# A kernel's own verdict counted by a product with ones, and two evictions moved from ScalarE to VectorE

## The chip, the cores and the metric

The kernel runs on one core of a Trainium2 chip. The metric is the device time of one execution in microseconds, as a median of several runs. A profile is of one execution; its span runs from the first to the last instruction of the program.

## What is computed

The reference is a gated linear recurrence (GateLoop) followed by a two-layer block with the activation h cos(h):

```python
# q, k, v, a_re, a_im: (4, 8, 768, 48); the state S is complex, per head 48 x 48
mag = np.sqrt(a_re * a_re + a_im * a_im)
scale = np.minimum(mag, 0.999) / (mag + 1e-06)
for t in range(S):
    S = (a_re + i a_im)[t] * scale[t] * S + outer(k[t], v[t])
    y[t] = q[t] @ real(S)
x = y.transpose(0, 2, 1, 3).reshape(3072, 384)
h = x @ w_in                 # w_in (384, 2048)
out = (h * np.cos(h)) @ w_out  # w_out (2048, 384), out (3072, 384)
```

(The recurrence is written here in complex form; the reference keeps the real and the imaginary part apart.)

## The kernel before

The program holds two kernels. `fast_path` relies on properties of the inputs: no real part below zero, powers that stay in range, weights that are normal numbers, arguments of the cosine in a range. While it runs it keeps account of them. `general_path` relies on none. At the end one value, the flag, is 1 if the account shows that the fast path's output can't be relied on. A branch (`tc.If(late["taken"] > 0)`, line 1658) then runs the general path, which writes everything again; the other arm (line 1661) only makes the last store. With the inputs used here the flag is 0 and the general path doesn't run.

**Tiles and groups.** The 4 x 768 steps are cut into chunks of 128 steps, two chunks are a group, and there are 12 groups (`NG`). A group passes through logarithms and powers of the gates, a phase, stacked keys and queries, scores, outputs and states, the first layer (`mm1_sums`, tiles `hp`), the activation (`gate_sine` on ScalarE, `gate_product` on VectorE) and the second layer. From the third group on, the second layer is Strassen's form of a product of 2 x 2 blocks: `mixed` makes sums of blocks of the gate on VectorE (tile `s`), and `seventh` makes one of seven products.

**The seven products of the last group.** `products` issues them in the order p0, p1, p3, p2, p5, p4, p6, each in two halves (`part`). p0, p3 and p5 add up in one PSUM tile, `sum`, which is evicted after each of them; p1, p2, p4 and p6 have a PSUM tile `op` each, which VectorE multiplies by a factor and adds to one or two of the blocks c11, c12, c21, c22 of the output (tile `ot`). In the last group (g = `NG` - 1) c12 is the tile `rest`, which outlives the fast path, and p6 stands alone: p5's sum is evicted twice, into c22 and into c12, and p6 is added to c12 last (`alone`). c11 is stored by SyncE after p1 (line 1210), the lower half of the rows after p4 (line 1212), and c12 by ScalarE from within the branch's other arm (line 1215).

**The account and the verdict.** `least` (96 x 16) holds ones and zeros for the powers at the chunks' ends, `odd` (128 x 41 partial sums, zero if nothing is amiss) the gates and the weights, `wide` the sums of squares of h. `verdict` is a generator that `judged` resumes three times within the last group's products. Its first step reduces `least` to `low` (96 x 1, ones and zeros) and `odd` and `wide` to `even` (128 x 1, ones and zeros), and in the kernel before writes both into a line in DRAM (lines 1634 and 1636) and reads that line back into one partition (line 1638). Its second step takes the minimum of the line (line 1641), compares it (line 1644, the flag) and has each engine read the flag into a register (line 1646). Its third step ties TensorE's read to a place among the matmuls.

**What sets the order.** On TensorE every matmul is chained to the one before (`matmul`, line 686), so its order is that of the program. On the other engines a planner sets the order by what is ready and by program order; `behind(a, b)` forbids that `a` goes before `b` on their engine. So line 1641 stands behind `late["vector"]`, the last eviction by VectorE that was issued till then; ScalarE's read of the flag behind `late["scalar"]`; TensorE's behind `late["tensor"]`; the last add behind VectorE's read (line 1206); p4's store behind SyncE's read (line 1213), and c11's store behind the read of the line (line 1210). `weave` merges lists of steps by due times between 0 and 1. In the last call the products' fourteen halves are due at (i + 0.5) / 14; the verdict's first step comes at 0.10 (between the halves of p0), the second at 0.59 (between p2 and p5), the third at 0.78 (between the halves of p4).

Of the kernel before, what the change touches and what calls it, by code (L numbers as in the profile page):

```python
# [11 lines left out]
F32 = mybir.dt.float32  # L12
# [7 lines left out]
ALU = mybir.AluOpType  # L20
AX = mybir.AxisListType
# [466 lines left out]
def fast_path(ctx, tc, q, k, v, a_re, a_im, moe_w_in, moe_w_out, out, least, odd, wide,  # L488
# [7 lines left out]
    nc = tc.nc  # L496
    B, H, S, D = q.shape
    DM, DF = moe_w_in.shape
    C = 128
# [3 lines left out]
    NG = N // G  # L503
    D2 = 2 * D
# [17 lines left out]
    pa = ctx.enter_context(tc.tile_pool(name="pa", bufs=5, space=PSUM))  # L522
# [11 lines left out]
    late = {}  # L534
# [8 lines left out]
    def behind(ins, other):  # L543
        tc.add_manual_dep(ins.ins, other.ins.name, mybir.DependencyInfo(
            mybir.DependencyClass.NoSync, mybir.DependencyReason.DATA))
# [9 lines left out]
    def scalar_tile(value, name):  # L555
        t = consts.tile([C, 1], F32, name=name)
        nc.vector.memset(t, value)
        return t
# [33 lines left out]
    one_b = scalar_tile(1.0, "one_b")  # L592
# [91 lines left out]
    vector, scalar = Ordered(nc.vector, "vector"), Ordered(nc.scalar, "scalar")  # L684

    def matmul(out, **kw):
        chain(nc.tensor.matmul(out, **kw), "tensor")  # L687
# [446 lines left out]
    PLAIN, HJ, E2 = 2, NJ // 2, DM // 2  # L1134
# [33 lines left out]
    scale = 1.0 / (in_scale * out_scale)  # L1168

    def left(g, name, j):  # L1170
        if name[0] == "s":
            return X[g]["mix"][j // 2][name][:, j % 2]
        half, i = int(name[2]) - 1, int(name[1]) - 1
        return X[g]["gate"][j // 2 + half * (HJ // 2)][:, j % 2, ts(i, C)]

    def seventh(g, p, part):


        x, name = X[g], SEVEN[p]
        if p == 0 and part == 0:  # L1180
            x["sum"] = pm.tile([C, E2], F32, tag="acc", name="sum", bufs=1)
            x["ot"] = [msb.tile([C, DM], F32, tag="ot", name="ot") for _ in range(G)]

        alone = g == NG - 1 and p == 6
        summed = p in (0, 3, 5, 6) and not alone
        if not summed and part == 0:
            x["op"] = pm.tile([C, E2], F32, tag="m", name="op", bufs=2)
        ps = x["sum"] if summed else x["op"]
        for j in range(part * HJ // 2, (part + 1) * HJ // 2):
            matmul(ps, lhsT=left(g, name, j), rhs=right[name][:, j],  # L1190
                   start=(j == 0 and (p == 0 or not summed)),
                   stop=(j == HJ - 1), skip_group_check=summed)
        if part == 0:
            return
        c11, c12, c21, c22 = (x["ot"][i][:, ts(half, E2)] for i in range(2) for half in range(2))
        if g == NG - 1:
            c12 = rest
        if p in (0, 3, 5) or p == 6 and not alone:
            late["scalar"] = scalar.mul(out={0: c11, 3: c21, 5: c22, 6: c12}[p], in_=ps, mul=scale)
        if g == NG - 1 and p == 5:  # L1200
            scalar.mul(out=c12, in_=ps, mul=scale)
        for part_ in {1: [c11], 2: [c21], 4: [c21, c22], 6: [c12] * alone}.get(p, []):
            added = vector.scalar_tensor_tensor(out=part_, in0=ps, scalar=scale,
                                                in1=part_, op0=ALU.mult, op1=ALU.add)
            if alone:
                behind(added, late["read DVE"])
            late["vector"] = added
        row = g * G * C
        if g == NG - 1 and p == 1:
            behind(nc.sync.dma_start(out=out[ds(row, C), 0:E2], in_=c11), late["line"])  # L1210
        elif p == 4:
            put = nc.sync.dma_start(out=out[ds(row + C, C), :], in_=x["ot"][1])
            behind(put, late["read SP"] if g == NG - 1 else late["ends"])
        elif p == 6 and alone:
            late["store"] = lambda: nc.scalar.dma_start(out=out[ds(row, C), E2:DM], in_=c12)
        elif p == 6:
            nc.sync.dma_start(out=out[ds(row, C), :], in_=x["ot"][0])

    def products(g, lo, hi):
        if g < PLAIN:  # L1220
            return []
        return [lambda p=p, part=part: seventh(g, p, part)
                for p in (0, 1, 3, 2, 5, 4, 6)[lo:hi] for part in range(2)]

    def mixes(g, lo, hi):
        return [lambda p=p: mixed(g, p) for p in range(lo, hi)] if g >= PLAIN else []
# [202 lines left out]
    even = even_steps(1, 0, G)  # L1429
# [101 lines left out]
    even = even_steps(2, 0, G)  # L1531
# [49 lines left out]
    for n in range(2, NG):  # L1581
# [6 lines left out]
              (keys(n + 1), *((0.5, 0.62) if n == PLAIN else (0.53, 0.64))),  # L1588
              (last_quarter() if n == PLAIN else [], 0.9, 1.0), (first(n), 0.56, 1.0),
              (mixes(n, 0, 2), 0.9, 1.0), (guarded(n - 1, per) if n > 3 else [], 0.0, 0.38))  # L1590
    checked = verdict(late, temp)

    def judged():
        late["tensor"] = tail["tensor"]
        next(checked, None)

    weave((mixes(NG - 1, 2, 4), 0.0, 0.1), ([judged], 0.05, 0.15),
          (products(NG - 1, 0, 7), 0.0, 1.0), ([judged], 0.58, 0.6), ([judged], 0.76, 0.8))
    assert not guards
    return late  # L1600
@with_exitstack
def kernel(ctx, tc, q, k, v, a_re, a_im, moe_w_in, moe_w_out, out):

    nc = tc.nc
    D2, H = 2 * q.shape[3], q.shape[1]
    keep = ctx.enter_context(tc.tile_pool(name="keep", bufs=1))
    least = keep.tile([D2, 2 * H], F32, name="least")
    C = 128  # L1610
    NG, NJ = q.shape[0] * q.shape[2] // C // 2, moe_w_out.shape[0] // C
    odd = keep.tile([C, moe_w_in.shape[0] // C * 4 + NJ + NG + 1], F32, name="odd")
    wide = keep.tile([C, NG * NJ // 2], F32, name="wide")
    rest = keep.tile([C, moe_w_out.shape[1] // 2], F32, name="rest")
    scratch = ctx.enter_context(tc.tile_pool(name="scratch", bufs=1,
                                             space=bass.MemoryType.DRAM))

    def behind(ins, other):
        tc.add_manual_dep(ins.ins, other.ins.name, mybir.DependencyInfo(
            mybir.DependencyClass.NoSync, mybir.DependencyReason.DATA))  # L1620

    def verdict(late, temp):

        low = keep.tile([D2, 1], F32, name="low")
        nc.vector.tensor_reduce(out=low, in_=least, axis=AX.X, op=ALU.min)
        even = keep.tile([C, 1], F32, name="even")
        nc.vector.tensor_reduce(out=even, in_=odd, axis=AX.X, op=ALU.max)
        most = keep.tile([C, 1], F32, name="most")
        nc.vector.tensor_reduce(out=most, in_=wide, axis=AX.X, op=ALU.max)
        nc.vector.tensor_scalar(out=even, in0=even, scalar1=0.0, scalar2=None, op0=ALU.is_le)  # L1630
        nc.vector.tensor_scalar(out=most, in0=most, scalar1=2.4, scalar2=None, op0=ALU.is_le)
        nc.vector.tensor_tensor(out=even, in0=even, in1=most, op=ALU.mult)
        line_d = scratch.tile([D2 + C], F32, name="line_d")
        behind(nc.sync.dma_start(out=line_d[0:D2], in_=low.rearrange("p o -> (p o)")),
               late["x"])
        nc.sync.dma_start(out=line_d[D2:D2 + C], in_=even.rearrange("p o -> (p o)"))
        line = temp("Q")[0:1, 0:D2 + C]
        late["line"] = nc.sync.dma_start(out=line, in_=line_d.unsqueeze(0))
        yield
        bad = keep.tile([1, 2], F32, name="bad")  # L1640
        behind(nc.vector.tensor_reduce(out=bad[:, 0:1], in_=line, axis=AX.X, op=ALU.min),
               late["vector"])
        flag = keep.tile([1, 1], I32, name="flag")
        nc.vector.tensor_scalar(out=flag, in0=bad[:, 0:1], scalar1=0.5, scalar2=None,
                                op0=ALU.is_lt)
        reads, values = nc.values_load_multi_w_load_instructions(
            flag[0:1, 0:1], min_val=0, max_val=1,
            skip_runtime_bounds_check_because="a comparison gives 0 or 1")
        late["taken"] = values[0]
        for ins in reads:  # L1650
            name = str(ins.ins.engine).split(".")[-1]
            late["read " + name] = ins
        behind(late["read Activation"], late["scalar"])
        yield
        behind(late["read PE"], late["tensor"])

    late = fast_path(tc, q, k, v, a_re, a_im, moe_w_in, moe_w_out, out, least, odd, wide, rest, verdict)
    with tc.If(late["taken"] > 0) as taken:
        general_path(tc, q, k, v, a_re, a_im, moe_w_in, moe_w_out, out)
    with taken.Else():  # L1660
        late["store"]()
# [30 lines left out]
```

## Time and profile before

| what | us |
|---|---|
| three runs: median (lowest to highest) | 660.77 (659.86 to 660.9) |
| the profiled execution | 660.9 |
| its span | 659.0 |
| TensorE busy | 643.3 (98%) |
| VectorE busy | 492.4 (75%) |
| ScalarE busy | 393.2 (60%) |
| mean granted TensorE clock | 0.999 of full speed |

The span is first instruction to last; the execution's time has 1.9 us around it. "Busy" is the share of the span in which an engine executes; reads of registers, branches, waits on semaphores and the issuing of DMAs are the sequencers' and not counted. An engine name with a q (SPq, ACTq) is such a sequencer's row. A row of the timeline has start, duration, engine, line, operation, `out<-in`, shapes, a count of merged instructions, and in brackets the idle time of the engine before it with what ended it. Matmuls overlap: one of 128x192 in f32 is two instructions of 0.327 us that start 0.163 us apart. Line 687 is the helper that issues every matmul, and line 676 the one that issues most operations of VectorE and ScalarE, so one goes by tile names.

### The profile page before, as it was taken

The numbers are of one execution on the slowest core, as the hardware profiler recorded it, in microseconds if no ns is written. First come the engines' busy times: TensorE is split into PE (matmuls) and PEld (weight loads), VectorE is DVE, ScalarE is ACT, GpSimd is POOL, SyncE is SP. The second block draws the span as 40 slices with busy tenths as digits, with TensorE's granted clock in tenths as the row PEclk, the third lists the DMA queues.
The fourth block names the chain that finished last, engine by engine and source line by source line (L and its number), as shares of the span: only waits on it lengthen the run. The fifth ranks groups of instructions, "written<-read, shape, count | busy, mean of one in ns | idle before, by whom it ended". The sixth has DMA issues, their size and how long they took to land.

```text
span 659.0 us, 10778 instructions
## 1 busy us (share of the span) xinstructions
PE 643.3 (98%) x4075; PEld 577.6 (88%) x4075; DVE 492.4 (75%) x799; ACT 393.2 (60%) x726; POOL 44.9 (7%) x72
## 2 busy tenths in 40 slices
PE   8999999999999999999999999999999999999996
PEld 6888877768889999899889899899898999999896
DVE  6999999788687687696787786876877878862251
ACT  7888686374673593594494495485485476433230
POOL 4010200000000000010010010000000010010000
PEclk9999999999999999999999999999999999999999
DMA  9967745636636656747738728737737743362101
GB/s 246 243 184 191 244 142 135 152 85 153 147 73 151 161 146 145 192 120 170 191 102 188 189 76 186 200 84 177 200 92 161 197 123 93 124 140 77 49 1 31
DMA packets 228312, 94.90 MB, mean 144 GB/s; under 512 B 208701, under 2 KB 217406, under 8 KB 228250
## 3 DMA queue, kind: packets, MB, share of 16 engines
q1 hardware_dynamic: 217720, 57.50, 39.4%
q0 software_dynamic: 8816, 36.51, 17.2%
q8 instruction: 34, 0.56, 0.4%
q10 hardware_dynamic: 1714, 0.11, 0.2%
q14 instruction: 28, 0.23, 0.1%
HBM read 69.28 MB, written 24.81 MB: 143 GB/s over the span
## 4 chain that ended last, share of the span: by engine, by line
PE 85%; DMA 4%; ACT 4%; DVE 4%; issue 1%; SPq 1%; DVEq 0%; POOLq 0%
PE hp L687 35%; PE op L687 16%; PE sum L687 15%; PE yp L687 6%; PE sc L687 5%; PE sp L687 4%; PE phs L687 2%; DMA x<-yT 1%; PE lgs L687 1%; DVE mag L676 1%; DMA kT<-moved 1%; DVE lo L676 1%; ACT tan L707 1%; PE yr L687 1%; PE tp L963 1%; DMA moved<-tr 1%
## 5 line engine op out<-in xcount | busy, mean ns | idle before, releaser
L687 PE MATMUL hp<-xT,w_in 128*128 128x256 f32 (+1 forms) x1176 | 252.6, 375 | 0.9 <-DMA xT<-x 0.9
L687 PEld LDWEIGHTS hp<-xT,w_in 128*128 128x128 f32 x1176 | 220.0, 190 | 31.0 <-issue 1.3
L707 ACT ACTIVATE gate<-hp,half_pi_b 128x512 f32<-128x512 f32 x96 | 66.0, 687 | 119.8 <-PE hp L687 119.8
L687 PE MATMUL op<-w_out,gate 128*128 128x192 f32 (+1 forms) x448 | 100.7, 375 | 0.0
L676 DVE TENSOR_TENSOR gate<-hp,gate 128x512 f32<-128x512 f32 x96 | 65.6, 683 | 46.9 <-ACT junk L676 46.8
L687 PEld LDWEIGHTS op<-w_out,gate 128*128 128x128 f32 x448 | 76.0, 190 | 16.8 <-issue 2.0
L687 PE MATMUL sum<-t_s,s 128*128 128x192 f32 x320 | 57.8, 330 | 0.0
L676 ACT ACTIVATE junk<-hp 128x512 bf16<-128x512 f32 x96 | 56.6, 590 | 0.0
L687 PEld LDWEIGHTS sum<-t_s,s 128*128 128x128 f32 x320 | 52.1, 190 | 1.5 <-issue 1.5
L687 PEld LDWEIGHTS sc<-qT,kT 96*128 96x128 f32 x384 | 48.2, 192 | 4.0 <-DMA qT<-moved 1.2
L687 PE MATMUL sc<-qT,kT 96*128 96x128 f32 x384 | 50.3, 277 | 1.3 <-DMA kT<-moved 0.8
L676 DVE SCALAR_TENSOR_TENSOR ot<-op,ot 128x192 f32<-128x192 f32 x40 | 13.3, 353 | 48.7 <-PE op L687 47.1
L676 DVE TENSOR_TENSOR atm<-sc,causal 128x512 f32<-128x512 f32 x48 | 32.8, 686 | 22.1 <-PE sc L687 22.1
L676 ACT ACTIVATE ot<-sum 128x192 f32<-128x192 f32 x39 | 12.6, 322 | 54.0 <-PE sum L687 53.8
L687 PE MATMUL yp<-atm,v 128*48 128x128 f32 x352 | 33.6, 277 | 0.9 <-DVE atm L676 0.9
L703 ACT ACT_TABLE_LOAD x24 | 30.8, 1283 | 1.1 <-PEq L1676 0.7
L676 ACT COPY yT<-yp 48x512 f32<-48x512 f32 x44 | 25.3, 574 | 8.2 <-PE yp L687 7.6
L687 PEld LDWEIGHTS sp<-v,ks 128*96 128x96 f32 x320 | 30.0, 165 | 0.1
L687 PE MATMUL yp<-qT,state 96*48 96x128 f32 x304 | 29.7, 272 | 0.0
L687 PE MATMUL sp<-v,ks 128*96 128x48 f32 x320 | 29.7, 246 | 0.0
L687 PE MATMUL sum<-w_out,gate 128*128 128x192 f32 x160 | 29.2, 327 | 0.0
L676 ACT CAST tan<-phs 128x384 int32<-128x384 f32 x24 | 11.4, 481 | 29.4 <-PE phs L687 29.4
(149 smaller groups left out, 1000.6 us busy)
## 6 DMA issues: line engine op xcount, KB each, us to landing
moved<-tr SPq DMA_DIRECT2D x20, 768.0 KB
raw<-in_moe_w_in_dram POOLq DMA_DIRECT2D x16, 768.0 KB, 5.2
raw<-in_moe_w_out_dram POOLq DMA_DIRECT2D x16, 768.0 KB, 4.7
kT<-moved SPq DMA_DIRECT2D x40, 192.0 KB
qT<-moved POOLq DMA_DIRECT2D x9, 768.0 KB, 6.4
k<-in_k_dram SPq DMA_DIRECT2D x24, 192.0 KB
q<-in_q_dram SPq DMA_DIRECT2D x24, 192.0 KB
v<-in_v_dram SPq DMA_DIRECT2D x24, 192.0 KB
```

What stands on the lines that cost most here:

```text
L676: ins = getattr(self.engine, op)(**kw)
L687: chain(nc.tensor.matmul(out, **kw), "tensor")
L703: chain(nc.scalar.preload_act_table_set(table))
L707: chain(nc.scalar.activation(func=func, **kw))
L963: chain(nc.tensor.transpose(ps[:, h], X[g][name[0] + "s"][:, x0 + h].rearrange("p a d -> p (a d)"), ident), "tensor")
```

## The change

The verdict's line in DRAM goes. `low` is multiplied into the first 96 partitions of `even` on VectorE, and a product of `even` (128 x 1) with a column of ones (`one_b`) on TensorE counts the ones in it into a 1 x 1 PSUM tile, `good`. The flag is 1 if the count is below 127.5. The flag's comparison now has the place behind `late["vector"]` that the minimum had. The verdict's second step is due at 0.43 in place of 0.59, which is between p3 and p2. Of p5 in the last group, both evictions are VectorE's. c11's store is no longer tied to the line.

```diff
+        if g == NG - 1 and p == 5:
+            for out_ in c22, c12:
+                vector.tensor_scalar(out=out_, in0=ps, scalar1=scale, scalar2=None, op0=ALU.mult)
+        elif p in (0, 3, 5) or p == 6 and not alone:
-        if p in (0, 3, 5) or p == 6 and not alone:
             late["scalar"] = scalar.mul(out={0: c11, 3: c21, 5: c22, 6: c12}[p], in_=ps, mul=scale)
-        if g == NG - 1 and p == 5:
-            scalar.mul(out=c12, in_=ps, mul=scale)
...
         if g == NG - 1 and p == 1:
-            behind(nc.sync.dma_start(out=out[ds(row, C), 0:E2], in_=c11), late["line"])
+            nc.sync.dma_start(out=out[ds(row, C), 0:E2], in_=c11)
...
-    checked = verdict(late, temp)
+    def counted(even):
+
+        ps = pa.tile([1, 1], F32, tag="a", name="good")
+        matmul(ps, lhsT=even, rhs=one_b, start=True, stop=True)
+        return ps
+
+    checked = verdict(late, counted)
...
-          (products(NG - 1, 0, 7), 0.0, 1.0), ([judged], 0.58, 0.6), ([judged], 0.76, 0.8))
+          (products(NG - 1, 0, 7), 0.0, 1.0), ([judged], 0.42, 0.44), ([judged], 0.76, 0.8))
...
-    def verdict(late, temp):
+    def verdict(late, counted):
...
         nc.vector.tensor_tensor(out=even, in0=even, in1=most, op=ALU.mult)
-        line_d = scratch.tile([D2 + C], F32, name="line_d")
-        behind(nc.sync.dma_start(out=line_d[0:D2], in_=low.rearrange("p o -> (p o)")),
-               late["x"])
-        nc.sync.dma_start(out=line_d[D2:D2 + C], in_=even.rearrange("p o -> (p o)"))
-        line = temp("Q")[0:1, 0:D2 + C]
-        late["line"] = nc.sync.dma_start(out=line, in_=line_d.unsqueeze(0))
+        nc.vector.tensor_tensor(out=even[0:D2], in0=even[0:D2], in1=low, op=ALU.mult)
         yield
-        bad = keep.tile([1, 2], F32, name="bad")
-        behind(nc.vector.tensor_reduce(out=bad[:, 0:1], in_=line, axis=AX.X, op=ALU.min),
-               late["vector"])
+        good = counted(even)
         flag = keep.tile([1, 1], I32, name="flag")
-        nc.vector.tensor_scalar(out=flag, in0=bad[:, 0:1], scalar1=0.5, scalar2=None,
-                                op0=ALU.is_lt)
+        behind(nc.vector.tensor_scalar(out=flag, in0=good, scalar1=C - 0.5, scalar2=None,
+                                       op0=ALU.is_lt), late["vector"])
```

## The prediction

> **What bounds the kernel now.** I read the page first, then the chain of waits and the timeline of the last twenty microseconds, because every line of the diff acts there, and last the tiles `flag` and `rest` and SyncE's waits.
>
> ```profile
> PE 643.3 (98%) x4075; PEld 577.6 (88%) x4075; DVE 492.4 (75%) x799; ACT 393.2 (60%) x726; POOL 44.9 (7%) x72
> ```
>
> TensorE is busy for 98% of the span: what is added to its stream ahead of its last matmul is paid in full, and what the other engines do counts only if TensorE or the end waits for it. The chain of waits, cut to 640 to 660 us, shows where that stream stops:
>
> ```profile
> 640.99 2.60 PE sum L687 x16
> 643.59 2.60 PE op L687 x16
> 646.18 2.60 PE sum L687 x16
> 648.78 5.21 PE op L687 x32
> ...
> 654.09 0.36 DVE rest L676
> ```
>
> There is no gap: 16 matmuls take 2.60 us, 0.163 us each, in each of the products p3, p2, p5, p4 and p6, up to 654.00. Neither the old verdict nor the branch stops TensorE. So the change can win nothing before 654.00, only after it. The timeline from 646 us shows the verdict, the branch and the last store:
>
> ```profile
> 646.07 0.24 SPq L1638 DMA_DIRECT2D Q<-line_d  x1
> ...
> 648.82 0.33 ACT L676 ACTIVATE ot<-sum 128x192 f32<-128x192 f32 x1 [4.87 <-PE sum L687]
> 649.05 0.33 ACT L676 ACTIVATE rest<-sum 128x192 f32<-128x192 f32 x1
> 649.21 0.37 DVE L1641 TENSOR_REDUCE bad<-Q 1x1 f32<-1x224 f32 x1 [2.57 <-DMA Q<-line_d]
> 649.62 0.14 DVE L1644 TENSOR_SCALAR flag<-bad 1x1 int32<-1x1 f32 x1
> ...
> 651.42 0.62 DVE L676 SCALAR_TENSOR_TENSOR ot<-op,ot 128x192 f32<-128x192 f32 x2 [1.66 <-PE op L687]
> 652.07 0.34 SPq L1212 DMA_DIRECT2D out_dram<-ot  x1
> 654.09 0.36 DVE L676 SCALAR_TENSOR_TENSOR rest<-op,rest 128x192 f32<-128x192 f32 x1 [2.05 <-PE op L687]
> 654.48 1.09 ACTq L1215 DMA_DIRECT2D out_dram<-rest  x1
> ```
>
> The reader is to see that VectorE's last add waits for TensorE alone, and that ScalarE issues the last store 0.03 us after the add ends (654.45 to 654.48). ScalarE isn't late. The rows of the two tiles say how early it is:
>
> ```profile
> L1646 ACTq TENSOR_LOAD <-flag x1: 467/467/467, 649.8 to 649.8; - x1
> L1646 PEldq TENSOR_LOAD <-flag x1: 490/490/490, 650.9 to 650.9; - x1
> ```
>
> ```profile
> L1215 ACTq EVENT_SEMAPHORE  x1: 17/17/17, 652.9 to 652.9; - x1
> ```
>
> ScalarE reads the flag at 649.8, compares at 650.32 and stands at line 1215, in the branch's other arm, at 652.86. The add releases it at 654.45: a slack of 1.6 us. Last, SyncE's waits say what holds the end:
>
> ```profile
> SPq L1687 <- DMA out_dram<-rest: 1.2, 1, 1.2
> ```
>
> SyncE's closing waits stop for the last store's landing; its next row starts at 657.82, and some 1.15 us of barrier follow to 659.0. So the end is TensorE's last matmul, the add (0.36), the issue (1.09), the landing (2.25 from the issue's end), the barrier. The store's semaphore steps show the landing's shape: 14 of its 16 parts land by 656.89, the other two at 657.53 and 657.81. The packets show why these two could be late: TensorE's queue fetches 16 KB of program from 655.62 for 1.10 us, another queue 8 KB from 656.20 for 0.66 us, both while the store's packets run (656.08 to 657.27).
>
> **The change, part by part.**
>
> (1) *The product with ones on TensorE.* `counted` is one f32 matmul of 128x1 by 128x1. An f32 matmul is two instructions here (a product of eight tiles shows x16), so two are added, between p3 and p2, in the stream that has no gap. No row has one column. The nearest is `sp`, 128 rows by 96 columns of weights and 48 moving: 320 in 29.7 us busy, 0.093 us each, so 2 x 0.093 = +0.19 us. From below: the shortest distance between two starts of `sp` is 0.041, 2 x 0.041 = +0.08. From above: where the short `yp` products cut into a 128x192 stream (597.24 to 599.66), entry costs 0.256 against 0.163 and the two starts after the return 0.200 and 0.268; 0.093 + 0.037 + 0.105 + 2 x 0.098 (29.7 us by 304 for `yp` with the state) = +0.43. I take **+0.19**, because `sp` follows and precedes the wide products without such a handover.
>
> [...]
>
> (2) *Its wait for `even`.* VectorE gains one 128x1 operation (`low` into `even`): the same kind took 0.154 (L1632, from 639.35), so `even` is ready at about 639.50 + 0.15 = 639.65. The product is due when p3's last matmul has gone, at 643.4. Nothing on TensorE's path: 3.7 us of cover. If the cover went, TensorE would stand still with p2, p5, p4 and p6 behind the product, microsecond for microsecond.
>
> (3) *The flag.* It now waits for the product instead of line 1638's DMA: about 643.4 + 0.19 + the 0.2 us that the first ScalarE read of `sum` starts after the last matmul, 643.8 instead of 649.6. Behind it on VectorE stand p2's add (646.28), p5's two evictions, p4's adds and the last add; the first is due 2.4 us later. Cost 0. The reads by register (0.47 to 0.54 us) come 5.8 us earlier on ScalarE, GpSimd and SyncE; TensorE's keeps its place between p4's halves, at 650.9, and VectorE's stands in a gap of 2.4 us.
>
> (4) *What goes.* Three small DMAs on SyncE's queue (0.45, 0.33 and 0.24 us to issue) and the reduce of 0.37 us. Nothing on the chain waited for them. c11's store goes from 646.40 to about 641.5, behind p1's add (641.08 + 0.36); it moves the same 96 KB, and no other store is near. p4's store still follows p4's adds, at 652.07.
>
> (5) *p5's two evictions to VectorE.* 2 x 0.36 us (the 128x192 rows of VectorE that read PSUM: 0.349 to 0.358; ScalarE's were 0.33) from 648.8 to 649.6. VectorE is free until 651.42, p4's adds: 1.8 us of cover, cost 0. Without it, p4's store and the last add would move by at most 0.7 us, and the last add only if VectorE were still busy at 654.09.
>
> (6) *ScalarE sooner.* With the evictions gone its last work is p3's eviction (643.62 + 0.33). It reads at about 644.0, compares at 644.5 and, with the 2.45 us that the jump took before (650.32 to 652.77), stands at line 1215 at about 647 instead of 652.86. It then waits 7 us for the same add. Gain 0 at the store's start. The issue itself, 1.09 us, has one neighbour: SyncE's issue of the same shape (128 rows of 768 bytes, L1210) took 0.34. If the long issue were an after-effect of the jump, up to 0.75 us would go; but ScalarE had stood there for 1.6 us, so I take 0 and keep -0.75 as an end.
>
> [...]
>
> (7) *Program fetches at the end.* After each jump the packets show a fetch (ScalarE and GpSimd 651.24 and 651.35, SyncE 653.42), and some 0.6 to 0.7 us after the engine goes on, a second one: 653.42 and 653.72 after 652.77 and 653.02. SyncE took 3.18 us over its jump (652.46 to 655.64), against 2.45 and 2.67, with those second fetches beside its first; its own second is then the one at 656.20. Without them I expect SyncE about 0.5 us sooner, its second fetch off the store, and one of the two late parts in time: the landing falls from 657.81 to 657.53, **-0.28 us**. Bounds: 0, if it stays; -0.92 (657.81 to 656.89), if both late parts come in.
>
> Sum: +0.19 - 0.28 = -0.09 us, against this execution's 660.9 us (span 659.0, and 1.9 around it). That execution is 0.13 above the median of the three runs, 660.77, so the median of the new kernel should be 660.7 us.
>
> **The rivals.**
>
> *No tail gain.* SyncE's fetch stays on the store: 660.77 + 0.19 = 660.96, at most + 0.43 = 661.2. For it: SyncE's jump keeps its place after p4's store. Also the outcome if ScalarE's jump does not come sooner at all. 0.27.
>
> *The end of the store shrinks.* ScalarE's issue falls to SyncE's 0.34 (-0.75) and both late parts land by 656.89 (-0.92): 660.77 + 0.19 - 1.67 = 659.3. For it: the same shape costs a third on SyncE. Against: the slack before the issue, and TensorE's own fetch (655.62), which the change leaves in place. 0.08. One of the two alone gives 660.0 or 660.2; 0.07.
>
> *Slower: TensorE's program fetch on the last store.* Its fetches of 16 KB mostly take 0.9 to 1.3 us, but the one at 643.87 took 2.51. If the one at the end, over which a part of the store waits, takes that long, the end moves by 2.51 - 1.10 = 1.41 us more: 660.77 + 0.19 + 1.41 = 662.4. It decides once it runs over by about 1.1 us. For it: two instructions more and another jump order shift the fetches. Against: one such length. 0.08.
>
> **How the numbers follow.** The forecast has 0.50. The range takes the ends of the unknown costs: below 660.77 + 0.08 - 0.75 - 0.92 = 659.2; above 660.77 + 0.43, and half of the 1.04 us between the runs shown, 661.7; only the slower rival is left out. Faster or slower by over 0.2% (1.3 us, about what a measurement of this kernel can tell from no change) are the second and third rival alone: 0.08 and 0.08; the rest, 0.84, is within.
>
> **What would show it.** Right: no gap on TensorE, two short matmuls near 643.4, a flag near 643.8, ScalarE's wait at line 1215 near 647, its store 0.03 us after the add, and an end that lies 4.5 to 4.9 us after the last matmul. Step 1 is wrong if the distance from p3's to p2's first start grows from 2.60 by more than 0.43. Step 2 is wrong if TensorE idles before the product. Step 6 is wrong if line 1215 takes well under 1.09. Step 7 is wrong if two parts of the store still land 0.6 us after the rest. The prediction as a whole fails if the instruction order before 600 us changes, which no line of the diff asks for.

## The result

| | before | changed |
|---|---|---|
| median of 6 runs, us | 660.63 (659.78 to 661.47) | 667.81 (666.18 to 673.01) |
| the profiled execution, us | 660.9 | 673.0 |
| its span, us | 659.0 | 671.2 |
| TensorE busy, us | 643.3 | 651.2 |
| mean granted TensorE clock | 0.999 | 0.989 |

The changed kernel is slower: ratio 1.0119, with a 95% interval of 1.0085 to 1.0153. The forecast was 660.7 us, no change. The profiled execution of the changed kernel is the slowest of its six, 5 us over their median; it serves here for the order of things, and sizes are taken from the experiments.

The tail, where the prediction looked, did better in this trace than it had said. First the chain of waits of the changed kernel from 650 us; its columns are start, duration, and the work that the end hung on:

```profile
653.85 2.60 PE sum L687 x16
656.45 0.12 PE good L687 x2
656.57 2.80 PE op L687 x16
659.36 2.60 PE sum L687 x16
661.96 5.21 PE op L687 x32
...
667.20 0.36 DVE rest L676
```

The product, `good`, costs 0.12 us, and the product p2 behind it takes 2.80 in place of 2.60: +0.32 us together. (This chain goes by the ends of matmuls, which are modelled. By their starts the 0.20 us lie on both sides: the step into the product is 0.256 us and the second step behind it 0.267, where 0.163 is the rule.) The timeline of the same stretch shows the rest:

```profile
656.38 0.19 PE L687 MATMUL good<-one_b,even 128*1 128x1 f32 x2
...
656.60 0.15 DVE L1644 TENSOR_SCALAR flag<-good 1x1 int32<-1x1 f32 x1 [2.31 <-PE good L687]
...
662.00 0.36 DVE L676 TENSOR_SCALAR ot<-sum 128x192 f32<-128x192 f32 x1 [2.19 <-PE sum L687]
662.27 0.35 DVE L676 TENSOR_SCALAR rest<-sum 128x192 f32<-128x192 f32 x1
...
664.60 0.62 DVE L676 SCALAR_TENSOR_TENSOR ot<-op,ot 128x192 f32<-128x192 f32 x2 [1.98 <-PE op L687]
...
667.59 0.39 ACTq L1216 DMA_DIRECT2D out_dram<-rest  x1
```

The flag's comparison starts 0.03 us behind the product's end, the moved evictions end 2 us before p4's adds, and ScalarE's issue takes 0.39 us where it took 1.09. From the last matmul's start to the end of the span it is 4.39 us, before 5.36. (That is one trace of each. Of the eight traces of this study that have the whole changed tail, six have 4.38 to 4.61 us and two, e8 and e12, 5.99 and 6.08; the four with the old verdict have 5.29 to 5.70.) So the time was not lost here: it was lost before 650 us, where no instruction was changed. An engine-by-engine list of both programs shows the same instructions in the same order up to the verdict's. The queue table of the page says what differs. Its columns are packets, MB, and the time that the packets took as a share of 16 DMA engines over the span; before:

```profile
q1 hardware_dynamic: 217720, 57.50, 39.4%
```

and after:

```profile
q1 hardware_dynamic: 217462, 57.50, 45.1%
```

The same bytes in nearly the same packets (258 fewer, nearly all of 4 bytes) take more time: 16 engines times 0.394 times 659.0 us make 4,154 us, 16 times 0.451 times 671.2 make 4,843, or 17% more. By size, the inputs' packets of 192 bytes rose from a mean of 16.0 to 18.8 ns and kT's of 128 bytes from 13.5 to 17.7. Their medians (15 and 13 ns) are the same; a part of the packets takes about twice as long or more: one in five is over one and a half times the median, before 3 in 100. That starts in the first 10 us: of the 192 byte packets from 5 to 10 us, nine in ten took up to 15 ns before and up to 29 after. And the page's row of the scores shows who waits in the end (its last columns: busy time, mean ns, idle time before and what ended it); before, then after:

```profile
L687 PE MATMUL sc<-qT,kT 96*128 96x128 f32 x384 | 50.3, 277 | 1.3 <-DMA kT<-moved 0.8
L687 PE MATMUL sc<-qT,kT 96*128 96x128 f32 x384 | 52.4, 283 | 6.7 <-DMA kT<-moved 6.0
```

The idle time before the scores rose from 1.3 to 6.7 us, and what ended most of it is kT's DMA (0.8 and 6.0 us).

**What had moved.** The old verdict had a tile `bad` in the pool `keep`, 8 bytes that take up 32, and the diff drops it. Pools lie one behind the other in SBUF, so every tile allocated behind it moved 32 bytes down. In the programs' allocations `re` goes from byte 68992 of a partition to 68960, `kT` from 121344 to 121312. Before, every one of these tiles that a DMA writes in bulk began at a multiple of 128 (68992 = 539 x 128, 121344 = 948 x 128); after, none does. The other thing that fell away outside the verdict is the line in DRAM, 224 numbers of 4 bytes; it was the last of the program's allocations there.

### The profile page after: what moved, and what is told of

The parts are those of the page before. It is cut to its first block, busy times and chain, and to the rows that moved or that the text cites. A ratio compares the mean times of both kernels' runs of the same rounds, so it can differ in the third digit from the quotient of the medians.

```text
span 671.2 us, 10777 instructions
## 1 busy us (share of the span) xinstructions
PE 651.2 (97%) x4077; PEld 583.5 (87%) x4077; DVE 492.5 (73%) x801; ACT 393.6 (59%) x724; POOL 45.5 (7%) x72
## 3 DMA queue, kind: packets, MB, share of 16 engines
q1 hardware_dynamic: 217462, 57.50, 45.1%
## 4 chain that ended last, share of the span: by engine, by line
PE 73%; DMA 10%; DVE 6%; ACT 4%; SPq 3%; issue 2%; POOL 0%; DVEq 0%
PE hp L687 22%; PE op L687 17%; PE sum L687 14%; DMA kT<-moved 6%; PE yp L687 6%; PE sc L687 5%; PE sp L687 4%; DMA moved<-tr 3%; SPq L948 3%; PE phs L687 2%; PE lgs L687 1%; DVE mag L676 1%; DVE lo L676 1%; DVE qs L676 1%; DVE ks L676 1%
## 5 line engine op out<-in xcount | busy, mean ns | idle before, releaser
L687 PE MATMUL sum<-t_s,s 128*128 128x192 f32 x320 | 59.2, 335 | 0.0
L687 PE MATMUL sc<-qT,kT 96*128 96x128 f32 x384 | 52.4, 283 | 6.7 <-DMA kT<-moved 6.0
L676 ACT ACTIVATE ot<-sum 128x192 f32<-128x192 f32 x38 | 12.3, 325 | 51.8 <-PE sum L687 51.6
L687 PE MATMUL sum<-w_out,gate 128*128 128x192 f32 x160 | 30.8, 338 | 0.0
```

What stands on the lines that cost most here:

```text
L676: ins = getattr(self.engine, op)(**kw)
```

## The experiments

The theory: a DMA packet pays for each aligned line of 128 bytes that it touches in SBUF. The rivals: the DRAM line that went moved something in DRAM; the new instructions themselves; a step of 64 bytes in place of 128; or that any shift costs. For each kernel the table has the mean ns of the two kinds of packets, the time that TensorE spent up to the starts of the scores' matmuls (the sum of the distances from the matmul started before, from the trace), the share of queue q1, and the ratio to the kernel before on the same chip. That kernel took 659.63 us beside e1 to e4, 661.93 beside e5 to e8 and 662.35 beside e9 to e12; the times expected below are to be read against it.

| kernel | 192 B, ns | 128 B, ns | scores, us | q1 | ratio (95% interval) |
|---|---|---|---|---|---|
| before | 16.0 | 13.5 | 48.3 | 39.4% | 1 |
| changed | 18.8 | 17.7 | 56.4 | 45.1% | 1.0119 (1.0085 to 1.0153) |
| e1, changed, addresses of before | 15.9 | 13.4 | 47.9 | 39.4% | 0.9995 (0.9972 to 1.0019) |
| e2, before, all 32 lower | 19.3 | 17.7 | 55.5 | 45.9% | 1.0132 (1.0092 to 1.0173) |
| e3, changed, DRAM line back | 19.2 | 17.8 | 55.9 | 46.0% | 1.0133 (1.0093 to 1.0173) |
| e4, before, all 64 higher | 16.3 | 17.1 | 51.6 | 42.1% | 1.0075 (1.005 to 1.01) |
| e5, changed, inputs alone aligned | 16.1 | 16.6 | 53.3 | 41.6% | 1.0085 (1.0057 to 1.0113) |
| e6, changed, inputs alone 32 low | 18.9 | 13.6 | 49.8 | 42.9% | 0.9984 (0.9962 to 1.0007) |
| e7, changed, kT's pool alone off by 64 | 16.2 | 16.8 | 54.2 | 41.5% | 1.0089 (1.0061 to 1.0117) |
| e8, changed, inputs off by 64, rest by 128 | 16.0 | 13.7 | 49.8 | 39.8% | 0.9996 (0.9969 to 1.0022) |
| e9, e1 with ScalarE's evictions | 16.0 | 13.4 | 49.0 | 39.3% | 0.9963 (0.9939 to 0.9988) |
| e10, before, evictions on VectorE | 16.0 | 13.6 | 48.2 | 39.6% | 0.9990 (0.9962 to 1.0018) |
| e12, e1 once more | 15.9 | 13.5 | 48.0 | 39.3% | 0.9954 (0.9929 to 0.998) |

**e1, the changed kernel at the old addresses.** The flag's tile takes 64 bytes instead of 32.

```diff
-        flag = keep.tile([1, 1], I32, name="flag")
+        flag = keep.tile([1, 16], I32, name="flag")[:, 0:1]
```

> The changed kernel with the tile of the flag made 32 bytes larger, so that every later tile in SBUF has the address that it has in the kernel before (a multiple of 64 bytes where the changed kernel has an odd multiple of 32). Nothing else differs from the changed kernel. Theory of the addresses: the 7 us go, and the packets of 192 and 128 bytes are back at means of 16.0 and 13.5 ns; what is left is the tail's own change, +0.3 us for the product and about -1.2 us behind the last matmul as in the changed kernel's trace, so 659.5 to 660.7 us. Rival, DRAM: the line's 4 KB of DRAM that fell away moved something in DRAM; then this stays at 667 to 668 us. Rival, the new instructions themselves: also 667 to 668.

Measured: 658.8 us beside 659.63 for before. The whole loss is gone. The queue table of its page:

```profile
q1 hardware_dynamic: 217462, 57.50, 39.4%
```

It has the packets of the changed kernel and the time of before. The DRAM and the instructions are as in the changed kernel, so neither was the cause.

**e2, the kernel before at the new addresses.** Flag and minimum share a tile.

```diff
-        bad = keep.tile([1, 2], F32, name="bad")
+        pair = keep.tile([1, 2], I32, name="flag")
+        flag, bad = pair[:, 0:1], pair[:, 1:2].bitcast(F32)
...
-        flag = keep.tile([1, 1], I32, name="flag")
```

> The kernel before, verdict, branch and evictions untouched, but with the flag and the minimum in one tile of 8 bytes, so that every later tile in SBUF lies 32 bytes lower, at the changed kernel's addresses. Theory of the addresses: 666 to 669 us, means of the 192 and 128 byte packets near 18.8 and 17.7 ns from the first 10 us on. Rival, DRAM, and rival, the new instructions: 660.6 us as before, as the line in DRAM and all instructions are there.

Measured: 669.05 us. With no instruction of the change in it, the kernel before loses all that the changed one lost. Its waits of TensorE name the place; before, then e2:

```profile
PE sc L687 <- DMA kT<-moved: 0.8, 1, 0.8
PE sc L687 <- DMA kT<-moved: 6.0, 4, 2.4
```

Up to the scores TensorE spent 7.2 us more than before (55.5 against 48.3), of 8.0 us by which the span grew (667.0 against 659.0).

**e3, the DRAM line put back** in the changed kernel.

```diff
+        line_d = scratch.tile([D2 + C], F32, name="line_d")
+        behind(nc.sync.dma_start(out=line_d[0:D2], in_=low.rearrange("p o -> (p o)")),
+               late["x"])
         yield
         good = counted(even)
```

> The changed kernel with the DRAM tile of the line put back, and one small DMA that writes the first part of it at its old place; SBUF addresses stay those of the changed kernel. Theory of the addresses: 667 to 668.5 us, no help. Rival, DRAM: back at 660 to 661 us.

Measured: 668.89 us, no help. DRAM is out.

**e4, the kernel before, 64 bytes higher.**

```diff
-        flag = keep.tile([1, 1], I32, name="flag")
+        flag = keep.tile([1, 24], I32, name="flag")[:, 0:1]
```

> The kernel before with a flag tile 64 bytes larger, so that every later tile in SBUF lies 64 bytes higher: still multiples of 64, but the halves of 128 exchanged. If 64 bytes is the step that counts: 660.6 us within 0.2%. If any shift of the addresses costs, or if 128 bytes is the step: 663 us or more. Rival, DRAM: 660.6 us.

Measured: 665.04 us, 0.75% more. So multiples of 64 are not enough, and the two kinds of packets part: 128 byte packets are nearly as dear as at 32 (17.1 ns), 192 byte packets hardly differ from before (16.3). That is how the lines of 128 bytes that a packet touches would part them. From a multiple of 128, 128 bytes touch one line, and from any other start two. Runs of 192 bytes, one behind the other, touch two lines from 0 or 64, and two or three by turns from 32 or 96.

**e5 and e6, the two halves.** In e5 the inputs keep the addresses of before and all above them is off; in e6 the reverse. (Both on the changed kernel, e5 with e1's larger flag.)

```diff
+    gt.tile([C, 24], F32, tag="pad", name="pad_gt", bufs=1)   # e5: 96 bytes
+    gt.tile([C, 8], F32, tag="pad", name="pad_gt", bufs=1)    # e6: 32 bytes
```

> The changed kernel with the flag's tile 32 bytes larger (all addresses as before) and 96 bytes put in front of the gate pool: the inputs' tiles (192 byte packets) lie on multiples of 128 as before, everything above (kT, qT, tr, yT, xT, ot, the weights' raw tiles) has the offset from a multiple of 128 that it has in the changed kernel. Theory that a packet pays for each 128 byte line of SBUF that it touches: kT's 128 byte packets near 17.7 ns, the inputs' near 16; time 662 to 667 us, since the products wait for kT. Rival, the time came through the inputs' loads: 659 us.

> The complement: the changed kernel with 32 bytes put in front of the gate pool, so that the inputs' tiles stay 32 bytes low and all above has the addresses of before. Theory of the 128 byte lines: the inputs' packets near 18.8 ns (2.5 lines instead of 2), kT's near 13.5; time 659.5 to 663 us, less than in the complement. Rival, the time came through the inputs' loads: 666 to 669 us. If both halves give little, the loss needs both at once.

Measured: 667.39 and 661.7 us beside 661.93. The inputs' packets are as slow in e6 as in the changed kernel (18.9 and 18.8 ns), and that alone costs nothing that can be told from before: the inputs are loaded ahead, and none of the waits listed for TensorE in e6 is for them. What is above them costs 0.85%, most of the loss. The halves add up to less than the 1.2 to 1.3% of the whole; whether a part needs both at once is not shown, as the intervals are wide.

Two things blur these ratios. The changed kernel at the old addresses has 0.9995 and 0.9954 itself (e1, e12), so against that e6 could cost up to 0.3% and e8 up to 0.4%; in both the scores cost TensorE 1.8 us more than in e12 (49.8 and 48.0). And the granted clock differs between runs: seven of e5's ten show 0.991 to 0.996, and the three at 0.999 or 1.000 took 664.1 to 665.7 us, where the median of before's 21 runs at 0.998 or more is 661.7. So of e5's 5.5 us about half goes with the clock, an estimate from three runs.

**e7 and e8, 64 bytes in one place.** e7 shifts the pool of kT, qT, tr and yT by 64 and what follows by 128; e8 shifts constants, weights and inputs by 64 and the rest by 128.

```diff
+    ft.tile([C, 16], F32, tag="pad", name="pad_ft", bufs=1)    # e7, with e1's flag
+    msb.tile([C, 16], F32, tag="pad", name="pad_msb", bufs=1)  # e7
+    gt.tile([C, 16], F32, tag="pad", name="pad_gt", bufs=1)    # e8, with a flag of 32 words
```

> The changed kernel with the addresses of before, but 64 bytes in front of the pool of kT, qT, tr and yT and 64 behind it: that pool is 64 off a multiple of 128, all others are on one. Theory of the 128 byte lines: kT's packets touch two lines instead of one, mean near 17.1 ns, inputs' unchanged near 16; the 5 us that the shift of all tiles by 64 cost are here: 662 to 665 us. If 64 bytes is the step or the loss lay in another pool: 659 us.

> The changed kernel with constants, weights and inputs 64 bytes above their addresses of before and all else 128 above. Theory of the 128 byte lines: a packet of 192 bytes touches two lines from either start, and 128 is no shift at all: 658 to 660 us, inputs' packets near 16 ns, kT's near 13.5. If any shift of 64 costs, or a multiple of 128 is not enough: 661 us or more.

Measured: 667.69 and 661.3 us beside 661.93. The one pool carries the loss of e4 (5.8 us, where 5 were expected); inputs at 64 and everything else 128 higher cost nothing that can be told from before, with packets of 16.0 and 13.7 ns. So no shift costs as such; it is the offset from 128 that counts, and in kT's pool. TensorE's waits in e7:

```profile
PE sc L689 <- DMA kT<-moved: 3.3, 4, 1.3
...
PE sc L689 <- issue: 1.9, 1, 1.9
```

Whether kT alone would do it was not tried apart from qT, tr and yT; kT's are the only 128 byte packets in this pool, and the packets of 6144 bytes that are read from tr rose by 1% only (250.8 to 253.9 ns). The packets of 4096 bytes on GpSimd's queue, qT's among them, took 221.0 ns in e7 and as long in e8 (220.7), where that pool starts at a multiple of 128.

**e11, the packets by themselves.** A kernel that leaves out the whole computation: batches of DMAs into one tile, at five offsets, no other engine at work but for memsets.

```python
for off in (0, 16, 8, 24, 0):      # words: 0, 64, 32, 96, 0 bytes
    tile_ = big[0:96, ds(off, 2048)].rearrange("p (x f j) -> p x f j", f=4, j=32)
    ...  # 12 DMAs of kT's form; then the same with the inputs' form
```

> Computes nothing of the reference: only DMAs from q into one tile of SBUF that starts on a multiple of 128, first kT's form (96 partitions, 16 runs of 128 bytes), then the inputs' form (128 partitions, 8 runs of 192 bytes), each at offsets of 0, 64, 32, 96 and 0 bytes; then it stores zeros' worth of rows. Theory that a packet pays for the 128 byte lines it touches: 128 byte packets cheap at 0 alone and dearer, alike, at 64, 32 and 96; 192 byte packets alike at 0 and 64 and dearer at 32 and 96. Rival, 64 byte steps: 128 byte packets cheap at 0 and 64. Rival, it needs the traffic of the engines or of other queues: all offsets alike.

| mean ns of a packet at offset | 0 | 64 | 32 | 96 | 0 again |
|---|---|---|---|---|---|
| 128 bytes | 12.9 | 19.2 | 18.4 | 18.7 | 12.9 |
| 192 bytes | 15.6 | 15.5 | 18.6 | 22.3 | 16.4 |

The 128 byte row is as the theory has it: cheap at a multiple of 128, dearer alike elsewhere, with 64 no better than 32. The 192 byte row parts 0 and 64 from 32 and 96, as it should; that 96 is dearer than 32, with the same count of lines, is not explained. Nor does the count give the price: a packet of 128 bytes over two lines took 18.4 to 19.2 ns, one of 192 bytes over two lines 15.5 to 16.4. And not every packet pays: at 64, 32 and 96 seven in ten of the 128 byte packets, all of which cross a line's end, still took 14 ns or less. So the runs show which offsets are dear, and not how a crossing costs. A batch of 128 byte packets took 14.8 and 15.6 us from the first to the last at 0, and 16.3 to 17.0 at the other offsets: the packets overlap (q1's packets took 110.5% of the 16 engines' span on this run's page), and the whole slows less than their mean. It needs no other engine and no other queue: beside q1 the page has one packet of program, and beside the DMAs a memset of 2.0 us and four of 0.1.

These offsets move the place that is written, not the one that is read.

**e9 and e10, the change's halves**, both at the addresses of before: e9 is e1 with p5's evictions back on ScalarE, e10 is the kernel before with them on VectorE.

```diff
-        if g == NG - 1 and p == 5:
-            for out_ in c22, c12:
-                vector.tensor_scalar(out=out_, in0=ps, scalar1=scale, scalar2=None, op0=ALU.mult)
-        elif p in (0, 3, 5) or p == 6 and not alone:
+        if p in (0, 3, 5) or p == 6 and not alone:
             late["scalar"] = scalar.mul(out={0: c11, 3: c21, 5: c22, 6: c12}[p], in_=ps, mul=scale)
+        if g == NG - 1 and p == 5:
+            scalar.mul(out=c12, in_=ps, mul=scale)
```

(This is e9; e10 is its reverse on the kernel before.)

> The changed kernel at the addresses of before, with p5's two evictions back on ScalarE: the product and the earlier flag alone. Theory of the addresses: within 0.3% of before. For the last store: ScalarE's evictions end at the same distance from the last matmul as before, and its jump follows at once instead of waiting for the flag, so it stands at the store's line some 2.6 us ahead of it. If the length of the issue is what is left of some 2.7 to 3.1 us after the jump's end (1.62 + 1.09, 2.15 + 0.79, 2.51 + 0.59 in three runs), the issue takes 0.4 to 0.6 us. If the issue is long because the verdict goes over DRAM, 0.39 us; if because ScalarE made the evictions, 0.6 to 1.1 us.

> The kernel before, at its own addresses, with p5's two evictions on VectorE alone; the verdict still goes over DRAM. The flag stays at 649.6 and so does ScalarE's jump: it stands at the store's line 1.6 to 2.5 us ahead. Theory that the time since the jump sets the length of the issue: 0.6 to 1.1 us, and the time of before within 0.2%. If ScalarE's evictions made the issue long: 0.39 us and 0.5 us less than before.

Measured: 660.61 and 661.41 us beside 662.35. The product alone is 0.4% faster than before (0.3% had been expected at most), the evictions alone cannot be told from before. The store's issue in e9:

```profile
L1215 ACTq DMA_DIRECT2D out_dram<-rest x1: 390/390/390, 655.5 to 655.5; - x1
```

and in e10:

```profile
L1216 ACTq DMA_DIRECT2D out_dram<-rest x1: 1362/1362/1362, 653.1 to 653.1; - x1
```

ScalarE's evictions do not make the issue long: it is 0.39 us in all the kernels with the product, and 0.59 to 1.36 in the four with the verdict over DRAM. In those four it shrinks with the time that ScalarE had stood ready (1.19 us: 1.36; 1.61: 1.09; 2.14: 0.79; 2.49: 0.59), which fits something that ends 2.6 to 3.1 us after ScalarE stands. But e9 stood ready for 2.32 us, and by that row should have had some 0.7, not 0.39. So the long issue goes with the verdict over DRAM, as one of the expectations for e9 had it; by what way stays open.

**e12, e1 again**, to narrow its interval.

> The changed kernel at the addresses of before once more, the version that keeps the change and drops its side effect, to narrow its interval. By the traces of 10 kernels the product costs 0.32 us on TensorE and the end after the last matmul is 4.4 to 4.6 us in most instead of 5.3 to 5.7: 0.5 to 0.9 us less than before, a ratio of 0.9985 to 0.9995. If the end's gain was chance: 1.0005.

Measured: 659.51 us beside 662.35, ratio 0.9954. It is faster than before, which e1 had left open, and by more than expected. On this occasion the kernel before scattered from 659.75 to 666.73 over 29 runs, e12 from 658.61 to 663.31. Its lowest is 1.1 us under that of before, and e1's was 0.3 under; the +0.32 of the product and the shorter issue explain some 0.4 us (1.09 - 0.39 - 0.32). A part goes with the granted clock: it was 0.998 or more in 11 of e12's 12 runs and in 17 of before's 29, and among those alone the medians are 659.5 and 661.3 us, 1.8 apart in place of 2.8. The rest is not explained: e12's own trace shows no gain at the end, since its last store landed late (3.54 us after the issue's end).

## Why the prediction was wrong

The step that failed is the sentence that bounded the whole: "So the change can win nothing before 654.00, only after it". It was taken to say that nothing can be lost there either, and the sum has no term for it; the one sign of failure named for that stretch was "if the instruction order before 600 us changes, which no line of the diff asks for". The order did not change. What changed was where the tiles lie. Step (4), "What goes", counted three DMAs and a reduce, and did not count the tile that the reduce wrote. Its 32 bytes were worth 7 to 9 us: e1 puts them back and has the time of before, e2 takes them from the kernel before and loses the same. The slower rival, a program fetch of 2.5 us on the last store, had no part in it (that fetch took 1.27 us in the changed kernel's trace).

The price came about as follows, each link with its run. Without the 32 bytes kT's packets start off a multiple of 128, and take longer on the mean (13.5 to 17.7 ns in the changed kernel; e11: 12.9 to 18.4 ns and more, alone). kT lands later, and the scores on TensorE wait for it (e2: 6.0 us for kT, in all 7.2 us more up to the scores). The inputs' packets are slower too, but by themselves cost nothing that can be told from before (e6: 18.9 ns against 16.0, ratio 0.9984).

The clock adds to it: where TensorE had waited 2.4 us for kT at 177.9 us, e2's granted clock is 0.50 for 3.4 us, and the changed kernel's profile has two such spells of 6.8 us, at 178.0 and 505.7 us, next to waits of 2.5 us for kT and 1.3 us for VectorE. Half their length is what they can cost at most, an estimate: 1.7 us in e2, 6.8 us in the changed kernel's profile. Seven of the thirteen traces have a wait of 1.7 us or more near 177 us, and five of these have a spell there; the other six, with waits up to 1.35 us, have none. That the wait sets off the spell was not tried by itself.

By its own steps:

(1) The product: +0.19 taken, +0.32 measured, within the ends of 0.08 and 0.43. The reason given for the row of `sp`, that there is no handover, was wrong: the entry (0.256 us in place of 0.163) and the slow step behind (0.267) are those of the `yp` rows, 0.20 us together, and the product itself is 0.12.

(2) and (3) were right: `even` was ready at 652.55, 3.8 us before the product, and the flag's comparison held nobody up.

(5) was right: the evictions ended at 662.62, 2.0 us before p4's adds.

(6) was right that ScalarE gains nothing by standing ready sooner (7.5 us ahead, where 1.6 had done) and wrong on the issue: 0.70 us shorter, near the end of 0.75 that had been kept and not taken.

(7) is shown in part. The last part of the store landed 1.77 us after the issue's end in the changed kernel, against 2.24. Of the eight traces with the changed tail six have 1.77 to 2.00, the four with the old verdict 2.22 to 2.87; but e8 and e12, with the changed tail, have 3.45 and 3.54. In those two the last program fetch of 16 KB is the longest of all thirteen (1.56 and 1.63 us; 0.94 to 1.45 in the others), much as the slower rival pictured it. That the one delays the other is not shown, and one trace of each could not have told 0.28 us.

## What to carry to other kernels

Before a change is costed by its instructions, look at what it allocates: a tile that comes or goes moves all tiles behind it, and where DMAs write runs of 128 bytes, a start off a multiple of 128 made their mean time a quarter to a third longer in the kernels here (16.6 to 17.8 ns, against 13.4 to 13.7 on a multiple). A pad behind the small tiles keeps the bulk where it was, and such a pad is also the control for every comparison of two versions. When a page shows more time for the same packets and bytes of a queue, look at addresses before looking at instructions.

## What was not expected of the hardware

Packets of 128 bytes that are written to SBUF 32, 64 or 96 bytes past a multiple of 128 took 18.4 to 19.2 ns on the mean instead of 12.9 (e11), with nothing else running; 64 was no better than 32 or 96. The inputs' slower packets, for which TensorE did not wait, cost next to nothing (e6: 18.9 against 16.0 ns, ratio 0.9984), while a like slowdown of kT's, on the same queue q1, cost 0.9% (e7: 16.8 against 13.5 ns). The one-column product between two wide ones cost more in the handover than in itself: 0.12 us, and 0.20 in the step into it and the second step behind it (the changed kernel's trace). And the issue of one and the same store from ScalarE took from 0.39 to 1.36 us.
